# Earlier residual rows, fewer weight loads in a loop, half-size weight sums and a later LayerNorm in a fused attention and FFN kernel

## The chip, the cores and the metric

The kernel runs on one core of one Trainium2 chip. The metric is the time of one execution in device microseconds (us), lower is better. "The span" is the time of one profiled execution from its first to its last instruction; it is about 2 us shorter than the time that the metric counts. Engines are written as in the profile: PE (matmul), PEld (its weight loads), DVE (vector), ACT (scalar), POOL (GpSimd), SP (the engine whose queue issues all DMAs here).

## The reference

```python
# x: (1, 2048, 1024) bf16; wqkv: (1024, 3072); wo: (1024, 1024)
# W_gate, W_up: (1024, 3584); W_down: (3584, 1024)
def reference(A_x, A_wqkv, A_wo, B_x, B_W_gate, B_W_up, B_W_down):
    # linear attention, 32 heads of 32
    #   q, k, v = split(layernorm(x) @ wqkv)
    #   phi(t) = where(t > 0, t + 1, exp(t)) + 1e-6
    #   kv = phi(k)^T v ; z = sum phi(k)
    #   num = phi(q) kv ; den = phi(q) z + 1e-6 ; o = num / den
    h = x + o @ wo
    # FFN on layernorm(h): gate = g * (g > 0) ; ((gate * up) @ W_down)
    return h + ffn(layernorm(h))
```

(`B_x` is not used.)

## The kernel before

The kernel works on 16 tiles of 128 tokens. Its stages are, one after the other:

1. **Key/value stage.** LayerNorm of x (LN1: statistics on DVE, `rstd` on POOL, norm on DVE, transposition by DMA), keys with `phi`, values, and the sum `kv`. Tiles 0 to 3 use plain products (`kvp_piece`). From tile 4 on, pairs of tiles p = 2 to 7 use a Strassen scheme of seven block products (P1 to P7) for four: `k_group(p)`, then `v_group(p)`. It needs differences of weight blocks, which POOL makes for the values and the queries (`w_sums`, out of `pool_q`) and DVE for the keys.
2. **Query stage.** The same scheme for the queries.
3. **Output stage.** For each tile t: `a2(t)` multiplies by `kv` (the "num group" of 8 small matmuls) and divides, a DMA transposes o (`T3d`), four tiles later `a4` multiplies by `wo` (16 matmuls) and adds x. Tiles 0 to 7 also get their second LayerNorm here (LN2: two sums on ACT, a power on POOL, the norm on ACT, and a DMA transpose `T5d`).
4. **FFN** in two passes.

All instructions of an engine run in the order in which the program adds them. That goes for SP's queue as well: a DMA whose data is not ready holds up all DMAs behind it.

Statistics, `phi` and the place where POOL gets its weight sums (line 605 is `bn_stats`, 613 the `rstd`, 619 the norm, 634 and 637 the two DVE steps of `phi`):

```python
def ln_stats(src_full, src_chunk_bufs, name):
    # two bn_stats, one bn_aggr, one add of EPS, on DVE; then:
    PL.add("pool", lambda e: e.tensor_tensor(out=rstd[:, k, :], in0=ve[:, k, :], in1=neghalf[:],
                                             op=ALU.pow), ...)

def ln1_stats(st):
    i = st % NX1
    ln1_k[st] = ln_stats(x1[:, i, :], B_x1[i], "ln1_%d" % st)
    run(pool_q, {5: 5, 6: 5, 7: 3, 8: 3, 9: 2, 10: 2}.get(st, 3) if st >= 5 else 0)

def fin():                                        # of phi, after ACT's exp
    PL.add("dve", lambda e: e.tensor_scalar(out=Et[:, k, :], in0=Et[:, k, :], scalar1=1.0,
                                            scalar2=1e-6, op0=ALU.min, op1=ALU.add), ...)
    PL.add("dve", lambda e: e.scalar_tensor_tensor(out=dst_ap, in0=src, scalar=C1, in1=Et[:, k, :],
                                                   op0=ALU.add, op1=ALU.max), ...)
```

So `pool_q` is run down in batches, each right behind the `rstd` of a tile and therefore ahead of the next tile's `rstd`. One piece is a difference of two 128x512 blocks.

The pairs, with their hooks (a hook i runs ahead of the product i of its group):

```python
for p in range(WB // 2, NP_):                     # p = 2 .. 7
    def h_k3(p=p): ...                            # kv sums of the pair before; ln1_stats(2 * p + 5)
    def h_v1(p=p): ...                            # x_sums(p + 1): four DVE differences for the next pair
    def h_v2(p=p): ...                            # ln1_norm and transpose of tile 2 * p + 5
    def h_v5(p=p): ...                            # ln1_stats(2 * p + 6)
    def h_v7(p=p): ...                            # ln1_norm and transpose of tile 2 * p + 6
    k_group(p, {3: h_k3})
    v_group(p, {1: h_v2, 3: h_v1, 5: h_v5, 7: h_v7})
```

Tile 8's statistics and norm come even earlier, among the plain value products of tiles 1 and 3. The output stage:

```python
def a4(st):
    # 16 matmuls into two banks; then on DVE h = that + x2[:, st % NX2, :]      (NX2 = 3)
    if st + NX2 < NST:
        load_x2(st + NX2)                          # 256 KB, x rows of a later tile
    dma(sl_hs[hs], h_scr[st * P:(st + 1) * P, :], hsb[:, hs, :], "st_h_%d" % st, ...)
    if st >= TPP: return                           # TPP = 8
    # ACT: sum and sum of squares; POOL: five small ops, one of them a power

def a4_norm(st):
    # ACT: norm of hsb into xn, then
    dma_t(sl_tx[kx], hnT[:, :, st * P:(st + 1) * P], xn[:, kx, :], "T5d_%d" % st, ...)

LAG = NE                                           # 4
for t in range(NE, NST + LAG + 1):
    if LAG + 1 <= t < TPP + LAG + 1:
        a4_norm(t - LAG - 1)
    if LAG <= t < NST + LAG:
        a4(t - LAG)
    if t < NST:
        a2(t)                                      # ends with the transpose T3d of o
    if 5 <= t < 5 + NWG:
        load_w_next()                              # 512 KB of W_gate or W_up, six times
    if t >= 9:
        run(pool_t, 1)
    if 13 <= t < 17:
        s_sums()[t - 13]()                         # DVE: S3, S1, S2, S4 from hnT, all eight tiles
```

`s_sums()[0]`, called S3, reads the transposed LN2 of all eight tiles, so it waits for `T5d` of tile 7. It stands on DVE ahead of `h` of tile 10 and `o` of tile 14, and PE's num group of tile 15 needs the bank that `o` of tile 14 frees.

## Time and profile before

| before | |
|---|---|
| time, median of 3 | 770.56 us (770.49 to 771.11) |
| span of the profiled execution | 769.0 us |
| key/value pairs begin (P7 of the keys of p=2) | 40.01 us |
| query stage | 54.95 us long |
| output stage (first matmul with `wo`) | 184.97 us, 72.72 us long |
| FFN begins | 257.69 us |

The page says which engine is full. These are the engine line of its first part, and the PE clock in tenths over 40 slices of 19 us, of the kernel before:

```profile
PE 741.7 (96%) x3544; PEld 337.4 (44%) x3599; DVE 553.2 (72%) x1085; ACT 294.2 (38%) x502; POOL 75.9 (10%) x116
PEclk9989999999999999999999999999999999999999
```

PE is busy for 96% of the span, and from 257.69 us on its 512-column matmuls follow each other at 0.216 us. What a change ahead of the FFN can win is PE's waiting there, and the time in which its clock is low. PE's waits of the kernel before (line waited for, us in total, times, longest):

```profile
PE ps L592 <- DMA RE<-RE: 8.0, 5, 3.1
PE ps L592 <- DVE RE L637: 4.7, 1, 4.7
...
PE ps L592 <- DVE RE L979: 1.4, 1, 1.4
```

The first line is the transposes of o in the output stage; the second is one wait for a `phi`. The second, seen on three engines of the kernel before (start, us, engine, line, operation, tiles, and in brackets the idle time ahead of it with what ended it), DVE first:

```profile
46.89 1.36 DVE L619 TENSOR_SCALAR RXH<-RE,mv,rstd 128x1024 bf16<-128x1024 bf16 x1 [1.15 <-POOL rstd L613]
48.18 1.27 DVE L605 BATCH_NORM_STATS2 st<-RE 128x6 f32<-128x512 bf16 x2
...
49.80 0.84 DVE L634 TENSOR_SCALAR RX<-RX 128x512 bf16<-128x512 bf16 x1
50.67 0.69 DVE L637 SCALAR_TENSOR_TENSOR RE<-ps,RX 128x512 bf16<-128x512 f32 x1
```

```profile
42.68 3.67 POOL L728 TENSOR_TENSOR RW<-RAB,RW 128x512 f16<-128x512 bf16 x3
46.31 0.55 POOL L613 TENSOR_TENSOR rstd<-ve,neghalf 128x1 f32<-128x1 f32 x1
46.82 3.67 POOL L728 TENSOR_TENSOR RW<-RAB,RW 128x512 f16<-128x512 bf16 x3
```

```profile
45.70 1.03 PE L592 MATMUL ps<-RAB 128*128 128x512 bf16 x4
51.42 1.89 PE L592 MATMUL ps<-RW,RWG 128*128 128x512 f16 x4 [4.69 <-DVE RE L637]
```

DVE's norm of tile 8 at 46.89 waits 1.15 us for an `rstd` that POOL can only do after its batch of three sums. Then the norm takes 1.36 us; without POOL work beside it, such a norm takes 0.54 us. The statistics and the `phi` that PE needs stand behind it. PE's next four matmuls take 1.89 instead of 1.03 us: the clock record shows half speed from 50.32 for 6.83 us.

From 201 to 246 us, in the output stage, SP's queue runs without a pause. One loop iteration of SP in the kernel before:

```profile
208.05 0.52 SPq L498 DMA_DIRECT2D RE<-in_A_x_dram  x1
208.62 0.43 SPq L498 DMA_DIRECT2D h_scr<-RXH  x1
209.16 1.43 SPq L502 DMA_TRANSPOSE RE<-RE  x1
210.64 0.88 SPq L498 DMA_DIRECT2D RWG<-in_B_W_gate_dram  x1
211.56 3.00 SPq L502 DMA_TRANSPOSE RH<-RXH  x1
```

The next one starts at 214.66, 6.61 us later, while PE's work for one tile is 3.92 us. `RE<-RE` is the transpose of o, `RH<-RXH` that of LN2. The waiting is also visible on the DMAs. This is the output stage in the view of stretches (stretch, its length, then busy time and count of PE, PEld, DVE, ACT, POOL, then mean granted PE clock, DMA share, GB/s):

```profile
184.97:257.69 72.72, 62.84 (x344) 30.87 (x351) 46.48 (x63) 29.17 (x43) 20.09 (x48) 0.98 0.94 221
```

Yet the chain of waits of the kernel before, followed back from the end, names something else from 190 to 226 us, with the same steps every 4.89 us:

```profile
219.35 1.14 ACT RX L1011 x2
220.51 1.16 ACT RX L1014 x2
...
222.08 0.56 POOL s L1025
...
224.23 1.14 ACT RX L1011 x2
```

That is LN2: two sums on ACT, POOL's power, ACT's norm, and the next tile's sums behind that norm.

### The profile page before, as it was taken

The page shows a single profiled execution, that of the slowest core. Times are in us where ns is not written, and L with a number is a line of the kernel's source. Part 1 is how long each engine was busy: PE and PEld are TensorE (multiplying, and loading weights), DVE is VectorE, ACT ScalarE, POOL GpSimd, SP SyncE. Part 2 cuts the span into 40 slices and gives each one's busy share as a digit, 9 for nine tenths or more (in the row PEclk, how much of TensorE's full clock was granted, in tenths as well). Part 3 has the DMA queues.
Part 4 walks back from the last instruction along what each step waited for, and adds up shares of the span by engine and source line. Part 5 has one row for each costly group of instructions (what it writes and reads, how often), then busy time and mean ns, then how long its engine had stood idle before and what let it go on. Part 6 is the DMA issues. An engine that isn't in the chain of part 4 may idle for free.

```text
span 769.0 us, 10054 instructions
## 1 busy us (share of the span) xinstructions
PE 741.7 (96%) x3544; PEld 337.4 (44%) x3599; DVE 553.2 (72%) x1085; ACT 294.2 (38%) x502; POOL 75.9 (10%) x116
## 2 busy tenths in 40 slices
PE   8979999999977999999999999999999999999998
PEld 4434444344533444444444444444444444444443
DVE  7989975889746698888886756748676686653433
ACT  4335465655660254544545100024544545420000
POOL 2764500000252000000000001000000000000000
PEclk9989999999999999999999999999999999999999
DMA  9633102112999577665535799762231323026654
GB/s 309 183 93 73 41 15 88 64 28 39 231 255 260 186 222 231 178 190 169 164 114 179 214 252 286 229 218 87 79 109 56 110 76 89 1 69 178 207 186 140
DMA packets 160225, 113.38 MB, mean 147 GB/s; under 512 B 51504, under 2 KB 141360, under 8 KB 160176
## 3 DMA queue, kind: packets, MB, share of 16 engines
q1 hardware_dynamic: 160176, 112.75, 51.6%
q8 instruction: 28, 0.46, 0.2%
q14 instruction: 21, 0.17, 0.1%
HBM read 85.46 MB, written 15.73 MB: 132 GB/s over the span
## 4 chain that ended last, share of the span: by engine, by line
PE 79%; DVE 8%; ACT 5%; issue 3%; DMA 2%; POOL 2%; SPq 1%; DVEq 0%; ACTq 0%; POOLq 0%
PE ps L592 79%; DVE RX L634 1%; ACT RX L1014 1%; ACT RX L1011 1%; ACT ps L597 1%; DMA RE<-in_A_x_dram 1%; DVE RE L637 1%; ACT RX L630 1%; DVE st L605 1%; DVE RX L829 1%; SPq L498 1%; DVE RAB L637 1%; DVE RC L728 1%; DMA RE<-RE 1%; DVE RXH L619 1%
## 5 line engine op out<-in xcount | busy, mean ns | idle before, releaser
L597 ACT ACTIVATE ps<-ps 128x512 f32<-128x512 f32 x152 | 88.7, 583 | 176.6 <-PE ps L592 164.9
L592 PE MATMUL ps<-RC,RO 128*128 128x512 f16 x672 | 154.2, 379 | 0.0
L592 PE MATMUL ps<-RW,RAB 128*128 128x512 f16 (+1 forms) x685 | 151.1, 379 | 0.6
L592 PEld LDWEIGHTS ps<-RW,RAB 128*128 128x128 bf16 (+1 forms) x696 | 68.1, 98 | 82.2
L592 PE MATMUL ps<-RH,RWG 128*128 128x512 bf16 x435 | 103.0, 379 | 0.7
L592 PEld LDWEIGHTS ps<-RC,RO 128*128 128x128 f16 x672 | 65.7, 98 | 79.3
L597 ACT ACTIVATE RE<-ps 128x512 f32<-128x512 f32 x120 | 71.0, 597 | 76.7 <-PE ps L592 54.5
L592 PE MATMUL ps<-RC,RWG 128*128 128x512 f16 x296 | 70.7, 379 | 0.0
L1161 DVE TENSOR_TENSOR RAB<-ps,RAB 128x512 bf16<-128x512 f32 x28 | 19.4, 692 | 66.5 <-PE ps L592 66.3
L592 PEld LDWEIGHTS ps<-RH,RWG 128*128 128x128 bf16 x448 | 43.8, 98 | 52.9
L592 PE MATMUL ps<-RW,RE 128*128 128x512 bf16 x248 | 58.3, 386 | 9.0 <-DMA RE<-RE 8.0
L592 PE MATMUL ps<-RH,RO 128*128 128x512 bf16 (+1 forms) x242 | 58.3, 379 | 0.7
L597 ACT ACTIVATE RAB<-ps 128x512 bf16<-128x512 f32 x56 | 33.4, 597 | 62.1 <-PE ps L592 62.1
L592 PE MATMUL ps<-RAB 128*128 128x512 bf16 x215 | 52.6, 384 | 1.3 <-ACT RAB L681 0.7
L1092 DVE TENSOR_TENSOR RO<-RWG,RO 128x512 f16<-128x512 bf16 x108 | 45.4, 420 | 1.8
L592 PEld LDWEIGHTS ps<-RC,RWG 128*128 128x128 bf16 (+1 forms) x296 | 28.5, 98 | 35.7 <-ACT ps L597 2.2
L1168 DVE TENSOR_TENSOR RE<-ps,RE 128x512 f32<-128x512 f32 x56 | 38.7, 691 | 5.5 <-ACT RE L597 5.4
L613 POOL TENSOR_TENSOR rstd<-ve,neghalf 128x1 f32<-128x1 f32 x24 | 14.6, 607 | 282.6 <-DVE ve L610 282.6
L592 PEld LDWEIGHTS ps<-RW,RE 128*128 128x128 bf16 x256 | 24.7, 99 | 38.0 <-DMA RE<-RE 8.8
L605 DVE BATCH_NORM_STATS2 st<-RE 128x6 f32<-128x512 bf16 x48 | 30.7, 680 | 13.9 <-DMA RE<-h_scr 12.9
L1092 DVE TENSOR_TENSOR RO<-RWG 128x512 f16<-128x512 bf16 x108 | 40.6, 418 | 0.0
L1173 DVE TENSOR_TENSOR RE<-ps,RE 128x512 f32<-128x512 f32 x56 | 38.1, 681 | 0.0
(111 smaller groups left out, 795.7 us busy)
## 6 DMA issues: line engine op xcount, KB each, us to landing
RWG<-in_B_W_gate_dram SPq DMA_DIRECT2D x28, 512.0 KB, 3.6
RWG<-in_B_W_up_dram SPq DMA_DIRECT2D x28, 512.0 KB, 4.7
RW<-t_scr SPq DMA_DIRECT2D x56, 256.0 KB, 3.1
RW<-in_B_W_down_dram SPq DMA_DIRECT2D x42, 256.0 KB, 4.0
RE<-in_A_x_dram SPq DMA_DIRECT2D x31, 256.0 KB, 3.9
RW<-in_B_W_down_dram SPq DMA_DIRECT2D x14, 512.0 KB, 3.9
t_scr<-RW SPq DMA_DIRECT2D x14, 512.0 KB, 4.9
RAB<-in_A_wqkv_dram SPq DMA_DIRECT2D x8, 512.0 KB, 8.4
```

The source lines that it names most:

```text
L498: return PL.add("sp", lambda e: e.dma_start(dst_ap, src_ap), reads=reads, writes=writes, slot=slot, name=name)
L592: lambda e: e.matmul(out_ap, lhsT, rhs, start=start, stop=stop, skip_group_check=skip),
L597: PL.add("act", lambda e: e.activation(out=dst, in_=src, func=func), reads=reads, writes=writes, name=name)
L605: PL.add("dve", lambda e, c=c: e.bn_stats(out=st6[:, k, c * 6:(c + 1) * 6], in_=src_full[:, c * BCH:(c + 1) * BCH]), reads=[src_chunk_bufs ...
L613: PL.add("pool", lambda e: e.tensor_tensor(out=rstd[:, k, :], in0=ve[:, k, :], in1=neghalf[:], op=ALU.pow), reads=[B_ve[k], B_neghalf], wr ...
L619: PL.add("dve", lambda e: e.tensor_scalar(out=dst_ap, in0=src_full, scalar1=mv[:, k, 0:1], scalar2=rstd[:, k, :], op0=ALU.subtract, op1=AL ...
L630: PL.add("act", lambda e: e.activation(out=Et[:, k, :], in_=src, func=ACTF.Exp), reads=[src_buf], writes=[B_E[k]], name=name + "_exp")
L637: PL.add("dve", lambda e: e.scalar_tensor_tensor(out=dst_ap, in0=src, scalar=C1, in1=Et[:, k, :], op0=ALU.add, op1=ALU.max), reads=[src_bu ...
L1092: PL.add(eng, lambda e: e.tensor_tensor(out=Tring[:, k, j], in0=in0, in1=in1, op=ALU.subtract), reads=reads, writes=[B_T[k][j]], name="T%d ...
L1161: PL.add("dve", lambda e: e.tensor_tensor(out=hh[:, f1, 0:SBW], in0=bank(BA[1]), in1=r11[:, rr, :], op=ALU.mult), reads=[B_bank[BA[1]], B_ ...
L1168: PL.add("dve", lambda e, w=w: e.tensor_tensor(out=ftmp[:, 4 + w, :], in0=bank(BF_[w]), in1=ftmp[:, 2 + w, :], op=ALU.add), reads=[B_bank[ ...
L1173: PL.add("dve", lambda e, w=w: e.tensor_tensor(out=ftmp[:, 6 + w, :], in0=bank(BB[w]), in1=ftmp[:, w, :], op=ALU.add), reads=[B_bank[BB[w] ...
```

## The change

Its intent: (a) take the x rows of the first eight tiles into a free buffer during the query stage, so that eight 256 KB loads leave the loop of the output stage; (b) spread the six 512 KB weight loads over more of that loop, two of them behind its crowded part; (c) POOL's sums in pieces of 256 columns instead of 512, with smaller batches after tiles 5 to 8 (8, 5, 4, 5 halves where there were 10, 10, 6, 6 halves' worth); (d) statistics and norms of LN1 later: from tile 8 on every hook takes the tile before the one that it took (2p+4 and 2p+5 in pair p instead of 2p+5 and 2p+6), and the norm of tile 7 moves back a little too; (e) the values of pair p=2 by plain products, because the smaller batches have not finished the value sums by then.

```diff
+        x2e = RC[:].rearrange("p (a b) -> p a b", a=TPP)
+        def x2_slot(st):
+            return st if st < TPP else TPP + st % NX2
...
-            if st + NX2 < NST:
+            if TPP <= st and st + NX2 < NST:
                 load_x2(st + NX2)
...
-            run(pool_q, {5: 5, 6: 5, 7: 3, 8: 3, 9: 2, 10: 2}.get(st, 3) if st >= 5 else 0)
+            run(pool_q, {5: 8, 6: 5, 7: 4, 8: 5, 9: 5, 10: 5}.get(st, 7) if st >= 5 else 0)
...
-                pool_q += w_sums("pool", wv_, bw_v, tw_v, B_TWv, "TWv", 1)
+                pool_q += w_sums("pool", wv_, bw_v, tw_v, B_TWv, "TWv", 1, NW // 2)
...
-        pool_q += w_sums("pool", wq, bw_q, TWq, B_TWq, "TWq", 1)
+        pool_q += w_sums("pool", wq, bw_q, TWq, B_TWq, "TWq", 1, NW // 2)
...
-                if nt == NKV - 1 and st == 1:
+                if nt == NKV - 1 and st == 2:
                     ln1_norm(WB + 3)
                     T1d(WB + 3)
-                    ln1_stats(WB + 4)
-                if nt == NKV - 1 and st == 3:
-                    ln1_norm(WB + 4)
-                    T1d(WB + 4)
...
-                if 2 * p + 5 < NST:                  # h_k3; the hooks of v_group likewise
-                    ln1_stats(2 * p + 5)
+                if 2 * p + 4 < NST:
+                    ln1_stats(2 * p + 4)
...
             k_group(p, {3: h_k3})
+            if p == WB // 2:                         # four kvp_piece with the same hooks between them
+                ...
+                continue
             v_group(p, {1: h_v2, 3: h_v1, 5: h_v5, 7: h_v7})
+        run(pool_q, len(pool_q))
...
-                    for i in range(NX2):
+                    for i in range(TPP + NX2):
                         load_x2(i)
...
-            if 5 <= t < 5 + NWG:
+            if t in (5, 7, 9, 11, 18, 19):
                 load_w_next()
```

(Buffer bookkeeping, the body of `w_sums` and the four hooks are left out.)

## The prediction

> **What bounds it now.** TensorE: busy 741.7 of 769.0 us (page, part 1), 79% of the chain of waits. From 257.7 us on (FFN, timeline of PE) 512-column matmuls follow each other every 0.216 us without a gap. The first 257 us decide:
>
> 1. Key/value stage, 40-129 us. PE waits 4.7 us at 46.7 for a DVE phi (view of waits). DVE timeline: its LN norms wait in order for POOL's rstd, queued behind three weight sums of 1.2 us each, and ops of 0.29-0.46 us take 0.85-1.37 us beside POOL. The Trainium skill ("SBUF — State Buffer", Who interferes with whom) says such pairs exclude each other; the durations agree. After the wait 8 matmuls take 3.6 instead of 1.9 us: half clock. Pair p=2 takes 20.3 us, an undisturbed one 13.5, p=4 15.1. DVE has almost no idle time from 47 to 103 us.
> 2. Query stage, 129-185: gaps of 0.2-0.5 us, unchanged.
> 3. Output projection, 185-257.7: 72.7 us for 60.9 us of PE work (16 x 3.45 + 12 x 0.47). Waits of 8.0 us for o's transposes, 1.4 us for DVE, and a half-clock stretch.
>
> **The change.**
> - Direct v of p=2: 32 matmuls for 28, +0.86 us, but no weight sums or adds in front of PE.
> - Stats of tile 8 move behind k2's products, so phi no longer waits for that rstd; POOL batches after the stats of tiles 6-8 shrink (4-5 halves instead of 6-10). I estimate p=2 at 60 matmuls + kvacc = 13.4 us: -6.9 us.
> - Against it: more LN and POOL work (47 half pieces instead of 16 whole) falls into p=3-5. DVE work there, 46 us plus an estimated 7 of collisions, about fills the 54 us. I expect PE waits of 0-2 us, against 2.0 us before. Net for this stage: -7 us (-4 to -9).
> - Output stage: eight 256 KB x loads and half of the 512 KB weight loads leave the loop. SP issued without pause, an iteration per 5.3-6.8 us, DMA share 1.0-1.1, PE needing 3.92. After, I estimate 3.5-4.1 us of issue, about 4 of DMA.
> - But the chain of waits shows another limit from 190 to 226 us: LN2's two ACT sums, POOL's pow, ACT norm, 4.89 us per tile, eight tiles, untouched. The last norm ends 39.2 us after h0, its transpose lands some 4.5 us later, and DVE (in order) stands before sum S3 until then; h10, o14 and PE's last `num` group follow: at 238.5 instead of 243.4 us (estimate, old time base). So about 5 of 11.8 lost us return, less about 1.3 if the now single gap of about 4 us drops the clock: -3.7 us (-1 to -6).
>
> **Prediction: 759.9 us, 754.5 to 765. Faster by over 2%: 0.10; within 2%: 0.89; slower: 0.01.**
>
> **What would show it.**
> - The 4.7 us wait and the first half-clock stretch gone; p=2 about 13.4 us.
> - p=3-5 still DVE-bound: small PE waits on DVE/ACT, DVE without idle.
> - LN2's period still 4.89 us; SP idle in the loop; transpose waits under 1 us each and one wait of about 4 us before the last `num` group, released by DVE, behind a DVE wait for the hnT transpose.
> - FFN onwards unchanged (511 us).
>
> **What would make it wrong.** Half pieces cost more than half (rstd late, DVE behind in p=3-5): gain down to 4. No clock drop in the output stage, or transposes landing in 3.5 us: up to 3 us better.

## The result, and the profile after

| | before | after |
|---|---|---|
| time, median of 4 | 770.84 us (770.49 to 772.14) | 762.41 us (761.66 to 762.89) |
| ratio, 95% interval | | 0.9887 (0.987 to 0.9904) |
| span of the profiled execution | 769.0 | 761.0 |
| pairs p=2 to 7, us each | 20.34, 13.70, 15.14, 13.85, 13.49, 13.49 | 13.46, 13.49, 14.55, 15.65, 14.26, 13.49 |
| output stage begins | 184.97 | 180.03 |
| output stage, length | 72.72 | 69.66 |
| FFN begins | 257.69 | 249.69 |
| FFN to the end | 511.31 | 511.31 |

Ratios are computed as the mean time of one kernel's fast runs over the mean of the other's fast runs of the same rounds, so they are not quite the ratio of the medians. A pair is timed from PE's P7 of its key group to the P7 of the next one; p=7 ends at the query stage's first P7. The program got 1.1% faster, inside the 2% that count as the same. Of the 8.0 us in the profiles, 4.9 come ahead of the output stage and 3.1 from it; the FFN did not change.

The same lines of the page as above, for the kernel after:

```profile
PE 740.7 (97%) x3547; PEld 337.8 (44%) x3603; DVE 548.3 (72%) x1083; ACT 293.8 (39%) x500; POOL 84.5 (11%) x148
PEclk9999999999998999999999999999999999999999
```

PE's busy time hardly moved. POOL's grew by 8.6 us, 7.5 of them for the same weight sums in smaller pieces (40.1 us before, 47.6 after). The slice with a low clock moved from 38 to 58 us to 228 to 247 us. PE's waits after:

```profile
PE ps L602 <- DVE RE L989: 4.5, 1, 4.5
PE ps L602 <- ACT RX L607: 2.2, 2, 1.3
...
PE ps L602 <- DMA RE<-RE: 1.3, 1, 1.3
```

The 8.0 us for transposes of o shrank to one wait of 1.3 us, and the 4.7 us for `phi` is gone. A single wait of 4.5 us for the division of o took the first place (it had been 1.4 us), and waits for ACT in the key/value stage came up. PE's timeline of the kernel after shows where:

```profile
45.80 7.93 PE L602 MATMUL ps<-RAB 128*128 128x512 bf16 x35
...
95.53 1.04 PE L602 MATMUL ps<-RAB,RH 128*128 128x512 bf16 x4 [1.27 <-ACT RX L607]
...
224.62 3.63 PE L602 MATMUL ps<-RW,RE 128*128 128x512 bf16 x16
232.73 1.06 PE L602 MATMUL ps<-kvz,RAB 128*128 128x132 bf16 x8 [4.48 <-DVE RE L989]
233.59 7.64 PE L602 MATMUL ps<-RW,RE 128*128 128x512 bf16 x23
```

At 45.80 the kernel before had stopped; now 35 matmuls run through at full speed. At 232.73 the num group of tile 15 waits 4.48 us, and its eight matmuls then take 1.06 instead of 0.63 us: half clock again, from 231.39 for 6.83 us, as the view of stretches for exactly that time has it (columns as before, the clock is the third from the end):

```profile
231.39:238.22 6.83, 5.49 (x19) 2.52 (x20) 6.30 (x7) 0.00 (x0) 0.00 (x0) 0.50 1.06 288
```

The whole output stage after, in the same view:

```profile
180.03:249.69 69.66, 63.52 (x344) 31.42 (x351) 46.95 (x63) 29.18 (x43) 21.01 (x48) 0.95 0.80 186
```

The DMA share fell from 0.94 to 0.80, so the DMAs no longer fill the stage, but the mean clock fell from 0.98 to 0.95. Behind the wait stand SP, ACT and DVE. Two LN2 norms of ACT in the kernel after, then SP ahead of the last LN2 transpose, then DVE:

```profile
218.18 1.24 ACT L1047 ACTIVATE RXH<-RXH,s 128x1024 bf16<-128x1024 bf16 x1 [1.43 <-POOL s L1037]
...
223.07 1.24 ACT L1047 ACTIVATE RXH<-RXH,s 128x1024 bf16<-128x1024 bf16 x1 [1.43 <-POOL s L1037]
```

```profile
221.41 1.30 SPq L512 DMA_TRANSPOSE RE<-RE  x1
222.76 0.58 SPq L508 DMA_DIRECT2D RWG<-in_B_W_up_dram  x1
224.34 1.24 SPq L512 DMA_TRANSPOSE RH<-RXH  x1
```

```profile
228.13 1.60 DVE L1084 TENSOR_TENSOR RC<-RH 128x2048 f16<-128x2048 bf16 x1 [5.28 <-DMA RH<-RXH]
229.65 1.21 DVE L1008 TENSOR_TENSOR RXH<-ps,RE 128x1024 bf16<-128x1024 f32 x1
...
231.45 1.23 DVE L989 TENSOR_TENSOR RE<-ps,rden 128x1024 bf16<-128x1024 f32 x1
```

The norms are 4.89 us apart, as before; each waits 1.43 us for POOL. SP is idle from 223.34 until the last norm ends and then issues the transpose at once, at 224.34. DVE stands still for 5.28 us in front of S3, and `h` of tile 10 and `o` of tile 14 come only then.

The key/value stage gave a part back in pairs 4 to 6. What happens ahead of PE's wait at 95.53 in the kernel after is read on DVE (ACT's op waits 1.98 us for the second line shown):

```profile
92.03 0.99 DVE L629 TENSOR_SCALAR RXH<-RE,mv,rstd 128x1024 bf16<-128x1024 bf16 x1
...
93.73 1.11 DVE L647 SCALAR_TENSOR_TENSOR RE<-RX 128x512 bf16<-128x512 f32 x1
94.76 1.69 DVE L764 TENSOR_TENSOR RWG<-RAB 128x512 f16<-128x512 bf16 x2
```

POOL was busy with half pieces from 90.36 to 92.74 and from 92.88 to 96.18. Without POOL beside them the same three take 0.54, 0.69 and 0.76 us, as an experiment below shows.

### The profile page after: what moved, and what is told of

It is laid out like the page before. It is cut to its first block, busy times and chain, and to the rows that moved or that the text cites. A ratio compares the mean times of both kernels' runs of the same rounds, so it can differ in the third digit from the quotient of the medians.

```text
span 761.0 us, 10079 instructions
## 1 busy us (share of the span) xinstructions
PE 740.7 (97%) x3547; PEld 337.8 (44%) x3603; DVE 548.3 (72%) x1083; ACT 293.8 (39%) x500; POOL 84.5 (11%) x148
## 4 chain that ended last, share of the span: by engine, by line
PE 89%; DVE 5%; ACT 3%; issue 2%; DMA 1%; DVEq 0%; POOL 0%; ACTq 0%; SPq 0%; POOLq 0%
PE ps L602 89%; ACT ps L607 1%; ACT RX L640 1%; DVE RAB L647 1%; DVE RX L644 1%; DVE RX L839 1%; DVE RWG L764 1%; DMA RE<-RE 1%; ACT RXH L607 0%; DVE RE L900 0%; DVE RE L989 0%; DVE RXH L1008 0%; DVE st L615 0%; DVE rden L987 0%; DVE RXH L629 0%
## 5 line engine op out<-in xcount | busy, mean ns | idle before, releaser
L602 PE MATMUL ps<-RAB 128*128 128x512 bf16 x239 | 56.7, 379 | 1.3 <-ACT RAB L691 0.7
L1178 DVE TENSOR_TENSOR RE<-ps,RE 128x512 f32<-128x512 f32 x56 | 38.4, 691 | 5.0 <-ACT RE L607 5.0
L602 PEld LDWEIGHTS ps<-RH,RO 128*128 128x128 f16 (+1 forms) x256 | 24.5, 98 | 31.1 <-ACT RX L607 2.6
```

Source lines behind the costliest of these rows:

```text
L602: lambda e: e.matmul(out_ap, lhsT, rhs, start=start, stop=stop, skip_group_check=skip),
L1178: PL.add("dve", lambda e, w=w: e.tensor_tensor(out=ftmp[:, 4 + w, :], in0=bank(BF_[w]), in1=ftmp[:, 2 + w, :], op=ALU.add), reads=[B_bank[ ...
```

## The experiments

Twelve kernels were run, each beside runs of the kernel before on the same chip. Those named b_ start from the kernel before, those named a_ from the kernel after. All outputs are right.

| run | what it is | us, median | before, same chip | ratio (95%) | output stage, us |
|---|---|---|---|---|---|
| b_both | before + (a) + (b) | 766.83 | 770.95 | 0.9949 (0.9934 to 0.9964) | 68.54 |
| b_xrows | before + (a) | 766.01 | 770.95 | 0.9934 (0.992 to 0.9949) | 68.24 |
| b_wload | before + (b) | 768.66 | 770.95 | 0.9968 (0.995 to 0.9985) | 70.67 |
| b_norm | before, LN2 norm behind `a4` | 776.53 | 770.95 | 1.0066 (1.0047 to 1.0085) | 77.44 |
| a_norm | after, the same move | 763.14 | 770.90 | 0.9903 (0.9888 to 0.9919) | 70.49 |
| a_ssum | after, S sums three iterations later | 758.70 | 770.90 | 0.9845 (0.9826 to 0.9864) | 65.77 |
| a_twq | after, query sums out of p=3 to 5 | 761.36 | 770.90 | 0.9879 (0.986 to 0.9899) | 68.85 |
| a_whole | after with whole pieces, about the same amounts | 763.83 | 770.90 | 0.9916 (0.9899 to 0.9933) | 68.67 |
| a_lnearly | after without (d) | 764.06 | 771.18 | 0.9906 (0.989 to 0.9922) | 68.88 |
| a_vgroup | after without (e) and without the smaller batches | 762.63 | 771.18 | 0.9888 (0.9872 to 0.9904) | 68.87 |
| b_half | before + half pieces of (c), same amounts | 769.12 | 770.15 | 0.9985 (0.9971 to 0.9998) | 71.64 |
| best | after + what the others taught | 752.96 | 771.18 | 0.9771 (0.9754 to 0.9788) | 61.45 |

The last column is from one profiled execution each, and the number of half-clock stretches differs between executions of one kernel (mean clock 0.991 to 0.998 for the kernel before), so tenths of a microsecond in it mean little. In the kernel before it is 72.72, in the kernel after 69.66.

### The output stage

Theory A: before, SP's queue with the DMAs behind it held the stage; once (a) and (b) relieve it, LN2's chain of 4.89 us per tile is the floor, by way of S3. The rival: one of the two held it all along, the chain before as well, or the queue after as well.

**b_both, b_xrows, b_wload.** Parts (a) and (b) on the kernel before, together and alone. b_xrows takes the `x2` hunks of the diff, b_wload only this one, b_both takes both:

```diff
-            if 5 <= t < 5 + NWG:
+            if t in (5, 7, 9, 11, 18, 19):
                 load_w_next()
```

> The kernel before with the output-stage half of the change alone (x rows early, fewer weight loads). Theory A (after the change the LN2 chain of ACT and POOL, 4.89 us a tile, is the floor of the output stage): key/value stage unchanged with its 4.7 us wait; output stage 69-70 us instead of 72.7, one long PE wait before the last num group; total about 767.5. Rival R (the DMA queue alone was the limit): output stage 61-65 us, total 759-763.

> The kernel before with only the early x rows. Transfers per iteration fall from about 5.6 to 4.9 us of DMA time, just the period of the LN2 chain. Theory A: nearly the whole gain of both parts, 768 (within 1 us of b_both). Rival R: about 40% of the gain of both parts.

> The kernel before with only the fewer weight loads. Transfers per iteration fall to about 4.7 us on average. Theory A: again nearly the whole gain of both parts, 768. Rival R: about 60% of it. If the two single gains add up to that of both, A's floor is wrong.

Measured in the stage: 4.2 us gained by both, 4.5 by the x rows alone, 2.0 by the weight loads alone. The weight loads alone bring about half of what both bring (0.32 of 0.51% by the ratios), which is nearer to the 60% of the rival than to theory A's "nearly the whole gain"; this part of A missed. The x rows alone bring all of it, where the rival wrote 40%. The parts do not add up: something else limits as soon as one of them is done, as a new floor would. That the x rows alone do as well as both has a visible reason. In b_both PE's waits are collected into one of 4.48 us ahead of the num group of tile 15, followed by half clock. In b_xrows they are spread (2.19, 0.79, 1.54 and 1.79 us among others) and the clock stays up in this stage of the profiled execution. Others of b_xrows had a lower mean clock (0.993 to 0.998) at nearly the same time, so this is at most a part of the reason.

**b_norm.** On the kernel before, LN2's chain is shortened: ACT's norm of a tile now stands behind the next tile's sums and so no longer waits for POOL.

```diff
-            if LAG + 1 <= t < TPP + LAG + 1:
-                a4_norm(t - LAG - 1)
             if LAG <= t < NST + LAG:
                 a4(t - LAG)
+            if LAG + 1 <= t < TPP + LAG + 1:
+                a4_norm(t - LAG - 1)
```

> The kernel before, with LN2's ACT norm of a tile moved behind the sums of the next tile, so that ACT no longer idles 1.43 us a tile for POOL: the period can fall from 4.89 to PE's 3.92 us. Theory A: in the kernel before the queue of transfers was behind the chain anyway (last transpose issued 6 us after its norm), so this alone gains at most 1 us: 770-771. Rival C (the chain that the profile of before shows was already the limit): about 5 us, 765-766.

Both expectations missed: it got slower, by 0.66%, and the stage by 4.7 us. The chain did get shorter. ACT's norms came 3.92 us apart as long as the tiles arrived in time, and the last one began at 224.41. But the same move puts the two transposes next to each other in SP's queue, and it puts LN2's behind the store of a later tile's `h`. SP in b_norm:

```profile
222.75 3.95 SPq L502 DMA_TRANSPOSE RE<-RE  x1
...
240.11 1.46 SPq L502 DMA_TRANSPOSE RH<-RXH  x1
```

The second of two adjacent transposes held SP for up to 3.95 us, the last iterations took 5.6 to 7.6 us with SP never idle, and the last LN2 transpose was issued at 240.11, 14 us after its norm had ended. So in the kernel before the chain of waits named LN2's steps, yet shortening them in this way did not help: SP's queue held the transposes. The expectations had not counted that the move changes SP's order as well as ACT's. What a shorter chain would bring there with SP's old order was not run.

**a_norm.** The same diff on the kernel after, where theory A says that LN2's chain is now the floor.

> The changed kernel with LN2's ACT norm behind the sums of the next tile. Theory A (LN2's 4.89 us a tile is the floor after the change): period falls to about 3.9 us, the last LN2 transpose lands about 8 us earlier, DVE doesn't stand before S3, the 4.5 us wait of PE and the half-clock stretch go: 754-757 us. Rival B (as in b_norm, two transposes issued one right after the other cost issue time, so the queue of transfers is the limit as soon as the chain is shortened): 760-764 us.

Theory A's gain did not come; the rival's figure held. The norms came 3.92 us apart and the last began at 216.06 instead of 223.07, but its transpose was issued at 223.94, hardly earlier than the 224.34 of the kernel after. SP in a_norm:

```profile
223.94 1.63 SPq L512 DMA_TRANSPOSE RH<-RXH  x1
225.68 2.37 SPq L512 DMA_TRANSPOSE RE<-RE  x1
```

SP is never idle here from 196 us on, and its LN2 transposes are 4.0 to 4.8 us apart, 4.5 on average (the last four steps 4.5 to 4.8). In the kernel after, LN2's chain (4.89) sets the last transpose, as the idle SP ahead of it shows; but the queue follows so closely behind that taking the chain away alone wins nothing. The move changed SP's order again, so the run can't say what the chain alone would be worth with a faster queue or with the old order.

**a_ssum.** On the kernel after, the S sums go three iterations later, so that DVE no longer stands in front of S3 while PE needs `o` of tile 14. Neither the chain nor the queue is touched.

```diff
-            if 13 <= t < 17:
-                s_sums()[t - 13]()
+            if 16 <= t < 20:
+                s_sums()[t - 16]()
```

> The changed kernel with the four S sums three iterations later, so that DVE doesn't stand in order before the last LN2 transpose while h10 and o14 wait; LN2 chain untouched at 4.89 us. Theory A: PE's 4.5 us wait before the last num group and the half-clock stretch go, small waits on o's transposes (about 1 us each) stay: 755-758 us. Rival (the transposes of o are what PE would wait for anyway): 760-763 us.

758.70 us, the direction as written and slightly less than the size: the ratio went from 0.9887 to 0.9845, and the stage from 69.66 to 65.77 us. PE in a_ssum:

```profile
228.29 0.63 PE L602 MATMUL ps<-kvz,RAB 128*128 128x132 bf16 x8
231.58 8.59 PE L602 MATMUL ps<-RW,RE 128*128 128x512 bf16 x39 [2.66 <-DMA RE<-RE]
```

The num group of tile 15 comes at 228.29 with no wait, and in this profile there is no half-clock stretch in this stage (mean clock 0.997 to 1.0 in all executions of a_ssum, 0.995 to 0.997 in those of the kernel after). A wait of 2.66 us for a transpose of o is left. This shows that the 4.48 us wait, and the clock drop behind it, came from where S3 stands on DVE.

### The key/value stage

The theory: the large POOL batch and the norm and statistics of tile 8 ahead of `phi` made the wait of 4.7 us; and POOL's query sums, now spread over p=3 to 5, collide with DVE and make the new waits of pairs 4 to 6. The rivals: one part, such as the half pieces or the plain values, removed the first wait; and the later LN1 alone made the new ones.

**b_half.** The half pieces of part (c) alone on the kernel before, with twice the counts, so that the same amount of POOL work stands at the same places.

```diff
-            run(pool_q, {5: 5, 6: 5, 7: 3, 8: 3, 9: 2, 10: 2}.get(st, 3) if st >= 5 else 0)
+            run(pool_q, {5: 10, 6: 10, 7: 6, 8: 6, 9: 4, 10: 4}.get(st, 6) if st >= 5 else 0)
```

> The kernel before with POOL sums in half pieces alone, the same columns in the same places (10, 10, 6, 6 half pieces after the stats of tiles 5-8). If the 4.7 us wait of p=2 comes from norm 8 standing before the phi until a rstd that is queued behind a batch of sums, it stays above 3 us with its half-clock stretch: 768-770.5. If it comes from DVE ops being blocked by long POOL pieces, it falls under 2 us: 764-766.5.

A ratio of 0.9985, nearly nothing. PE still waits 3.5 us for the `phi` of p=2 and still gets half clock behind it. DVE in b_half, the norm of tile 8:

```profile
46.82 0.88 DVE L619 TENSOR_SCALAR RXH<-RE,mv,rstd 128x1024 bf16<-128x1024 bf16 x1 [2.43 <-POOL rstd L613]
```

The norm is blocked for less time (0.88 instead of 1.36 us), but it waits longer for `rstd`, 2.43 instead of 1.15 us, because six half pieces take 4.46 us where three whole ones took 3.67. The pair's 18.55 us in the table below says little: in the profiles of before, b_both, b_xrows, b_wload and b_norm, which all have the same code in this stage, it took 18.68 to 20.39.

**a_vgroup.** Part (e) undone: p=2 has its Strassen values back, and the counts give POOL enough halves in time. With that the smaller batches of (c) are undone too.

```diff
-            run(pool_q, {5: 8, 6: 5, 7: 4, 8: 5, 9: 5, 10: 5}.get(st, 7) if st >= 5 else 0)
+            run(pool_q, {5: 10, 6: 10, 7: 6, 8: 6, 9: 4, 10: 4}.get(st, 6) if st >= 5 else 0)
...
-            if p == WB // 2:
-                ...
-                continue
```

> The changed kernel with the Strassen v of p=2 back, for which POOL must have the v sums done as early as before (10, 10, 6, 6 half pieces after the stats of tiles 5-8); later LN kept. If taking norm 8 and stats 9 from in front of the phi is enough: wait in p=2 at most 1.5 us, 0.86 us of matmuls less, total 761.5-764. If the direct v is what takes the wait away: a wait of 3 us or more with a half-clock stretch, 766 or more.

**a_lnearly.** Part (d) undone: statistics, norms and transposes of LN1 where they were before, and the rest of the kernel after. (The diff moves each hook by one tile, not by the two of the expectation.)

```diff
-                if nt == NKV - 1 and st == 2:
+                if nt == NKV - 1 and st == 1:
                     ln1_norm(WB + 3)
                     T1d(WB + 3)
+                    ln1_stats(WB + 4)
+                if nt == NKV - 1 and st == 3:
+                    ln1_norm(WB + 4)
+                    T1d(WB + 4)
...
-                if 2 * p + 4 < NST:                  # h_k3; the hooks of v_group likewise
-                    ln1_stats(2 * p + 4)
+                if 2 * p + 5 < NST:
+                    ln1_stats(2 * p + 5)
```

> The changed kernel with the LN1 hooks two tiles early again, as before (direct v, half pieces and small POOL batches kept). If the small batches and the direct v take away the 4.7 us wait, and the later LN only loads p=4-6: no long wait in p=2, pair p=5 shorter, total 760.5-762.5, equal or up to 1.5 us better than the changed kernel. If the later LN took the wait away: a wait of over 3 us and a half-clock stretch in p=2 again, 766 or more.

**a_whole.** The half pieces of (c) undone: whole pieces again, in counts that keep about the same amounts.

```diff
-            run(pool_q, {5: 8, 6: 5, 7: 4, 8: 5, 9: 5, 10: 5}.get(st, 7) if st >= 5 else 0)
+            run(pool_q, {5: 4, 6: 3, 7: 2, 8: 2, 9: 3, 10: 2}.get(st, 4 if st % 2 else 3) if st >= 5 else 0)
...
-                pool_q += w_sums("pool", wv_, bw_v, tw_v, B_TWv, "TWv", 1, NW // 2)
+                pool_q += w_sums("pool", wv_, bw_v, tw_v, B_TWv, "TWv", 1)
...
-        pool_q += w_sums("pool", wq, bw_q, TWq, B_TWq, "TWq", 1, NW // 2)
+        pool_q += w_sums("pool", wq, bw_q, TWq, B_TWq, "TWq", 1)
```

> The changed kernel with POOL sums in whole 512-column pieces, in the same places (half the counts). If the half pieces matter, DVE ops blocked by POOL take 0.9 us longer again instead of 0.4, and p=3-6 lose 1-3 us more: 763.5-765.5. If only the placing of the sums matters: within 0.7 us of the changed kernel.

These four go together. The pairs p=2 to 7, in us:

| | p=2 | p=3 | p=4 | p=5 | p=6 | p=7 |
|---|---|---|---|---|---|---|
| before | 20.34 | 13.70 | 15.14 | 13.85 | 13.49 | 13.49 |
| after | 13.46 | 13.49 | 14.55 | 15.65 | 14.26 | 13.49 |
| b_half | 18.55 | 14.03 | 14.99 | 13.49 | 13.49 | 13.49 |
| a_vgroup | 14.90 | 13.67 | 15.01 | 15.07 | 13.49 | 13.49 |
| a_lnearly | 13.46 | 16.28 | 14.69 | 15.30 | 13.49 | 13.49 |
| a_whole | 13.46 | 13.49 | 15.79 | 16.07 | 13.49 | 13.49 |
| a_twq | 13.46 | 13.49 | 13.48 | 13.49 | 13.49 | 16.39 |
| best | 13.46 | 13.49 | 13.49 | 13.49 | 13.49 | 15.99 |

The pair p=2 takes 13.46 us with the half pieces or part (d) taken away, and 14.90 with part (e) and the smaller batches taken away. So the change removes the first wait more than once over, and no single part of it can be called the cause. b_half, with the early norm of tile 8, the large batches and the Strassen values, keeps the wait. a_vgroup differs from it here by the later LN1 alone, and loses all but 1.4 us; so the later LN1 is enough. a_lnearly has the early norm, the smaller batches (five halves after tile 6, four after tile 7) and the plain values, and loses the wait as well, but p=3 then takes 16.28 us, so a part of the delay may only be put off. No run takes the batch size and the plain values apart there, but its trace says much: DVE's norm of tile 8 starts at 43.24 instead of 46.89 us, and the `phi` behind it ends at 47.01 instead of 51.36. No plain value product of p=2 stands ahead of them on DVE, and half pieces alone left that norm at 46.82 (b_half), so these 4.35 us, nearly the whole wait, come from the smaller batches. a_vgroup also says that the plain values are not needed: its ratio, 0.9888, is the same as that of the kernel after (it waits 1.1 us for POOL's sums in p=2 and loses less later). The later LN1 is worth something elsewhere: without it, p=3 takes 16.28 us, the six pairs take 1.8 us more, and the time rises by about 1.5 us by the ratios (their intervals overlap). The expectation of an equal or better time missed. Whole pieces cost about 0.3% by the two ratios, whose intervals overlap slightly. The profiles show 0.9 us more in the six pairs, with two waits of PE for ACT of 2.0 and 2.1 us, in p=4 and 5, where the kernel after has 0.9 and 1.3. So the half pieces seem to be worth a little, though POOL's own time grows.

**a_twq.** The query sums, the part of POOL's work that the kernel after does in p=3 to 5, are moved behind everything, into the key group of p=6.

```diff
-            run(pool_q, {5: 8, 6: 5, 7: 4, 8: 5, 9: 5, 10: 5}.get(st, 7) if st >= 5 else 0)
+            run(pool_q, {5: 8, 6: 5, 7: 4, 8: 5, 9: 5, 10: 5}.get(st, 0) if st >= 5 else 0)
...
                 if 2 * p + 4 < NST:
                     ln1_stats(2 * p + 4)
+                if p == NP_ - 2:
+                    run(pool_q, len(pool_q))
```

> The changed kernel with POOL's 32 half pieces of the query sums after the last LN1 tile (pair p=6 on) instead of in p=3-5. If collisions of DVE with POOL together with the later LN make DVE late in p=4-6 (pairs 14.6, 15.7, 14.3 us against 13.5 undisturbed), these pairs fall to 13.5-14 and the total to 759-760. If the later LN alone fills DVE, the pairs stay within 0.5 us of the changed kernel's.

Pairs 3 to 6 all fall to 13.48 or 13.49 us, with the later LN1 still in place. The same three DVE instructions of p=5 as above, in a_twq:

```profile
89.76 0.54 DVE L629 TENSOR_SCALAR RXH<-RE,mv,rstd 128x1024 bf16<-128x1024 bf16 x1
...
90.53 0.69 DVE L647 SCALAR_TENSOR_TENSOR RE<-RX 128x512 bf16<-128x512 f32 x1
91.14 0.76 DVE L764 TENSOR_TENSOR RWG<-RAB 128x512 f16<-128x512 bf16 x2
```

They take 1.99 us together instead of 3.79. That shows that the waits of pairs 4 to 6 come from POOL's sums beside DVE, not from the later LN1 by itself. The median gains only 1.0 us (the intervals of the two ratios overlap widely) and misses what was written by more than 1 us, because the loss reappears where the sums went: the last slot takes 16.39 us, with waits of 1.03 us for ACT and 1.24 us for DVE.

### A version that beats both

**best.** The kernel after, with the S sums late as in a_ssum; with the LN2 norm behind `a2`, which shortens ACT's chain and leaves the transpose of o ahead of LN2's in SP's queue; with two more weight loads out of the early iterations; and with the query sums in small portions up to p=5 and the rest at the end.

```diff
-            run(pool_q, {5: 8, 6: 5, 7: 4, 8: 5, 9: 5, 10: 5}.get(st, 7) if st >= 5 else 0)
+            run(pool_q, {5: 8, 6: 5, 7: 4, 8: 5, 9: 5, 10: 5}.get(st, 3) if st >= 5 else 0)
...
                     ln1_stats(2 * p + 4)
+                else:
+                    run(pool_q, 8 if p == NP_ - 2 else len(pool_q))
...
-            if LAG + 1 <= t < TPP + LAG + 1:
-                a4_norm(t - LAG - 1)
             if LAG <= t < NST + LAG:
                 a4(t - LAG)
             if t < NST:
                 a2(t)
-            if t in (5, 7, 9, 11, 18, 19):
+            if LAG + 1 <= t < TPP + LAG + 1:
+                a4_norm(t - LAG - 1)
+            if t in (5, 7, 13, 15, 18, 19):
                 load_w_next()
...
-            if 13 <= t < 17:
-                s_sums()[t - 13]()
+            if 16 <= t < 20:
+                s_sums()[t - 16]()
```

> The changed kernel with S sums three iterations later, LN2's norm and transpose behind o's transpose in the order of SP, the third and fourth weight load at t=13 and 15, and POOL's query sums spread thin (3 half pieces a tile, 8 and the rest in p=6 and p=7). Theory: no wait before the last num group, waits on o's transposes under 2 us in all, pairs p=4-6 within 1.5 us of undisturbed in all: 751.5-755. If the queue of transfers stays the limit (rival of a_norm): 756-759.

752.96 us, 2.3% below the kernel before and 1.2% below the kernel after by the two ratios. Its output stage in the view of stretches (columns as before):

```profile
178.16:239.61 61.45, 61.02 (x352) 30.56 (x353) 45.76 (x62) 29.20 (x43) 20.10 (x48) 1.00 0.90 210
```

PE is busy for 61.02 of 61.45 us at full clock, so nothing is left to win there without doing less work. What is left ahead of it is 2.5 us in the last slot of the key/value stage. Several things were changed at once in this run, so it does not say what each was worth.

## Why the prediction was right, and where its sum was off

The prediction of 759.9 us (754.5 to 765) met 762.41 us: the range and the class held, and most of the mechanisms were the ones the traces showed. It was 2.5 us too low, and the terms tell where.

- **p=2.** Predicted 13.4 us, a gain of 6.9. Measured 13.46, a gain of 6.88; the 4.7 us wait and the half clock behind it are gone. Right in size. The reason given, the norm and statistics of tile 8 ahead of `phi` behind a large batch, agrees with b_half, which keeps them and the wait, with a_vgroup, which moves them and keeps large batches, and with the trace of a_lnearly, where smaller batches alone bring `phi` 4.35 us forward. What the prediction did not see is that the parts are redundant: the plain values could have been left out.
- **The mis-sized term: pairs 3 to 5.** "I expect PE waits of 0-2 us, against 2.0 us before." Above the undisturbed 13.49 us, the pairs p=4 to 6 lost 1.06, 2.16 and 0.77 us after the change, 4.0 us in all (3.2 in the three pairs p=3 to 5 that the prediction named), where they had lost 1.65, 0.36 and 0.00, 2.0 us, before. So the stage's net, with p=3 and the small differences at its ends, was 4.9 us ahead of the output stage instead of 7. a_twq shows the cause: POOL's query sums beside DVE. The estimate that DVE's work with 7 us of collisions "about fills the 54 us" was an average over a long stretch (54 us are four undisturbed pairs, not the three named), but the waits come where a burst of sums meets the few DVE instructions that PE needs next. "DVE without idle" missed too: in p=3 to 5 DVE was busy for 39.6 of 43.7 us.
- **DVE and POOL exclude each other.** The Trainium skill ("SBUF — State Buffer", Who interferes with whom) says that a two-port DVE instruction contends with GpSimd, that a DVE instruction with two SBUF inputs contends with GpSimd reads, and that the second one blocks for the whole instruction. The traces agree: the norm takes 0.54 us alone, 0.88 to 0.99 beside half pieces and 1.36 beside whole ones; the DVE difference of two SBUF tiles takes 0.76 for two alone and 1.69 beside POOL. The `phi` step that reads PSUM takes 0.69 us in either case. (The prediction's 0.29-0.46 us for undisturbed operations is too low for the norm.)
- **Half pieces.** The prediction named "half pieces cost more than half" as a risk, and it came true: POOL's mean for RW<-RAB,RW is 1.18 us for 512 columns and 0.69 us for 256. An estimate from these two is about 0.2 us per instruction that does not shrink; the shortest of each, 1.15 and 0.67 us, give the same. POOL's busy time rose from 75.9 to 84.5 us. The gain is that each block of DVE is shorter; b_half and a_whole put the balance between 0.1% and 0.3% of the time, not well clear of noise.
- **The output stage, its floor.** Predicted: LN2's period stays 4.89 us, SP gets idle, the transposes of o stop being late, and one wait of about 4 us stands before the last num group, behind S3. All of that is in the trace: 4.89, SP idle for 1.0 us ahead of the last LN2 transpose, one wait of 1.3 us for o (the prediction said under 1), and 4.48 us before the num group of tile 15.
- **Its size.** Predicted -3.7 us, measured -3.1. The num group of tile 15 came earlier than predicted: relative to the stage's start it gained 5.7 us (58.43 to 52.70), against the 4.9 of the prediction. The clock drop took more: from that group to the FFN the kernel after needs 16.96 us and the kernel before 14.29, so 2.7 us came back instead of the estimated 1.3. (One profiled execution of each; the clock records of the other three of the kernel after, 0.995 to 0.997, allow a smaller cost in some.) So the sum came close to the measured one partly by luck: 0.8 us more gained and 1.4 us more lost. a_ssum, which removes the wait, has no drop and gains 3.9 us in the stage.
- **SP's iteration.** The estimate of 3.5 to 4.1 us of issue was about right for the kernel after: without SP's idle time its loop iterations from 191.83 to 220.73 took 3.3 to 4.5 us, 3.8 on average. It does not hold for every order. In a_norm, where ACT no longer holds the transposes and the two are adjacent, an iteration took 4.5 us on average, close to the chain's 4.89, and so the run that should have shown the chain's worth showed nothing.
- **The reading of the chain of waits.** The prediction took LN2's chain as a limit beside SP's queue in the kernel before. b_norm shows that in the kernel before this move of the norm did not relieve it: the norms came earlier there, and their transposes waited in SP's queue instead.

When the clock drops can be read off the kept traces. The Trainium skill ("TensorE: Matmul & The Clock Gate", Part 1: The HAM clock gate) gives half clock after at least one idle window of about 3.4 us, and a window that runs freely. The lengths agree: every half-clock stretch ahead of the FFN lasted 3.41 or 6.83 us, and the full-clock stretches between clock changes were whole multiples of 3.413 us too (in the kernel before 13, 48 and 160 of them). The length of a wait does not decide: in b_norm the clock dropped behind waits of 2.09 and 2.13 us, and in a_ssum it did not behind 2.66 us. What separates the cases is how much PE works inside one window. Lay a grid of 3.413 us over each of the 14 profiles, from its first clock change on, and take PE's busy time in every window up to 275 us. At full clock, 18 windows had at most 1.32 us of it, and the clock halved at the end of each; all others had at least 1.50 us, and it halved after none of them. Two windows on either side of that border, of b_norm and of b_xrows, in the view of stretches:

```profile
217.74:221.15 3.41, 1.32 (x12) 0.74 (x11) 1.68 (x3) 0.69 (x2) 1.40 (x3) 1.00 1.14 233
218.73:222.14 3.41, 1.50 (x13) 0.84 (x11) 0.52 (x1) 2.36 (x5) 1.13 (x4) 1.00 1.21 204
```

The 2.66 us wait of a_ssum lies across two windows, which keep 2.22 and 1.95 us of work. A stretch went on for a second window where PE was busy for at most 2.52 us in the first (six times), and the clock came back after every half-clock window with 2.75 us or more. Where a wait falls on the grid is a matter of luck: the first clock change lies anywhere from 4.4 to 7.4 us in the 14 profiles. It is a reading of 14 traces, in which the ends of matmuls are modelled; no run shifted a wait to test it.

## What to carry to other kernels

When a change takes load off a saturated queue, look for the next limit close behind it and ask which in-order engine stands still because of it: here moving four DVE sums three iterations later was worth over a third as much as the whole change (0.42 and 1.13% by the ratios). Work on POOL is not free just because POOL is idle; place it where DVE's next instruction does not feed PE, and count a collision by the instruction it delays rather than by its average. The chain of waits names what came last, not what would help; before building on it, shorten the step it names and see.

## What the Trainium skill lacked or had wrong

- "TensorE: Matmul & The Clock Gate", Part 1: "after ≥1 idle window (~3.4µs)" does not say how much PE may work in a window that counts as idle. Here the clock halved after all 18 windows with up to 1.32 us of work and after none with 1.50 us or more. So it halved behind PE waits of 2.09 and 2.13 us (b_norm) and 3.09 us (before, at 220.98), and stayed full behind 2.19 us (b_xrows) and 2.66 us (a_ssum). The lengths of the stretches, 3.41 and 6.83 us, agree with its window.
- "DMA: Bandwidth & Descriptors", DMA Transpose (X-bar): it gives no time for which a transpose of a 128x1024 tile holds the issuing queue (elsewhere the page has cycles in the sequencer for transposes, without a duration for this shape). Here it was 1.23 us where nothing stood in the way, 1.4 to 3.4 us in the full queue of the kernel before, and up to 3.95 us right behind another transpose (b_norm). Of those right behind another in a_norm, the four with a 512 KB weight load three or four issues ahead took 1.94 to 2.37 us and the four others 1.23 to 1.25, so a neighbour alone is not the cause, and the weight load is the likelier one; no run tested it.
- "GPSIMD Engine Reference", 3.1 Elementwise: it names a dispatch step for GpSimd without a duration (2.1 has "tens of cycles" for one part of it). The two sizes here, 1.18 us for 512 columns and 0.69 us for 256, give an estimate of about 0.2 us per instruction.
- "SBUF — State Buffer", Who interferes with whom, agreed with the traces: 0.54 us alone and 1.36 us beside POOL for the same DVE norm.
